# Re-ordering the start of an attention and feed-forward kernel: early scores, split zero fills, spreads ahead of a product, two more accumulator banks

## The chip, the cores and the metric

The kernel runs on one core of one Trainium2 chip. The metric is the device time of the whole program in microseconds, lower is better. A profile is one recorded execution of it; its times count from the first instruction of the span.

## What is computed

Causal attention over 4 batches, 8 heads, 768 positions and a head width of 64. Three heads ("retrieval", 0, 2 and 6) see all earlier keys. The other five ("streaming") see the first 4 keys (the sinks) and the last 64. The result, as a matrix of 3072 tokens by 512, goes through two matrix products with a leaky ReLU between them:

```python
scores = scale * np.matmul(q, k.transpose(0, 1, 3, 2))
mask = np.where(retr[0, :, 0, 0, None, None], full_mask, stream_mask)
scores = np.where(mask[None, :, :, :], scores, -1000000000.0)
a = np.exp(scores - np.max(scores, axis=-1, keepdims=True))
a = a / (np.sum(a, axis=-1, keepdims=True) + 1e-09)
attn_out = np.matmul(a, v)
x = np.ascontiguousarray(attn_out.transpose(0, 2, 1, 3)).reshape(B * S, H * D)
h = x @ w_in
out = np.maximum(0.01 * h, h) @ w_out
```

## The kernel before

The 3072 tokens are cut into eight chunks of 384 (`CH`), two for each batch. A chunk goes through three stages: attention, product 1 (`in_slots`: 16 ticks of four matmuls into a `ph` bank, evacuated by ACT with the leaky ReLU at L431) and product 2 (`out_slots`: three tiles of 128 tokens with 16 matmuls each, in parts of 3 or 4, copied by DVE at L447 and stored by SP).

The order on each engine is written out by hand. There is no scheduler that moves an instruction: the order of the Python calls is the order in which each engine gets its instructions. The tile layer adds a wait on a semaphore wherever an instruction touches data that another engine writes or reads, going by the regions that both touch. Each engine takes its instructions in that order, so one that waits holds all behind it.

Names used below:

- `kt[i]` holds the keys of a batch transposed, one plane for each pair of heads and each half of the pair (`hh`): the head's own 64 partitions hold keys, the other 64 partitions are zero, so that a matmul over all 128 partitions picks one head. `zero_keys` writes those zeros, for both chunks of the batch (768 positions). There are two such tiles, for batches in turn.
- Pairs: heads 0 and 1 are pair 0, and so on. R0, R2, R6 are the retrieval heads, S1, S3, S4, S5, S7 the streaming ones. `qk(*R0)` issues a head's score matmuls, its exponentials on ACT and its mask on DVE; `av(*R0)` multiplies by the values into an accumulator (`po` or `py` bank, by `po_tags`).
- `turn_pair(n, p, tags, engs)` transposes the keys and queries of pair p of chunk n on PE and copies them out of PSUM into `kt` and `qt` (L204 on DVE, L206 on ACT, by the letters `v` and `a`). Chunk 0's first two pairs come in fp32 by the DMA queues of SP and ACT (`kf`, `qf`); its other two come through Pool (`kw`, `qw`). Chunk 1's come through Pool (`kb`, `qb`) and are also turned on PE. From chunk 2 on the DMA transposes (`turn_dma`, into `kd` and `qd`), and `spreads` copies `kd` into `kt` on DVE (L228).
- `finish(p)` adds the sink part and normalises a pair on DVE into `xs` (L377, L379); `x_t` transposes `xs` on PE into `xt`, the input of product 1.
- `v_shift_pe` makes copies of the values shifted by 64 positions with a matmul by the matrix `shift`; `sink_keys`, `sink_values` and `a0.sink()` make the sink part.
- Pool issues the loads that convert to bf16 (`load_three`, `load_qk`, `load_v`, `load_in`, `load_out`) and builds the masks between them, all on one queue.

Chunk 0 runs alone at the start (`a0`). Then product 1 of chunk 0 (`p0`) and attention of chunk 1 (`a1`, slots of one score unit each, with its `av` two slots later and `x_t` three slots after the finish) are merged into one list. Product 1 of chunk 1 runs alone, then product 2 of chunks 0 and 1 (`o0`, `o1`) is merged with attention of chunk 2. From there a loop repeats the pattern for later chunks.

There are eight PSUM banks in four tags of two: `ph`, `psS`, `po`, `py`. A new tile of a tag waits until the one before the last of that tag has been read.

Of the kernel before, what the change touches and what calls it, by code (L numbers as in the profile page):

```python
# [13 lines left out]
ACTF = mybir.ActivationFunctionType  # L14
# [3 lines left out]
CH = 384  # L18
# [3 lines left out]
def kernel(  # L22
# [12 lines left out]
    nc = tc.nc  # L35
    B, H, S, D = q.shape
# [21 lines left out]
    def bf(name, *shape):  # L58
        return one.tile([128, *shape], BF16, name=name)
# [7 lines left out]
    ident = bf("ident", 128)  # L67
    ident_f = one.tile([128, 128], FP32, name="ident_f")
# [5 lines left out]
    shift = bf("shift", 2, 128)  # L74
    kt = [bf(f"kt{i}", 4, 2, S) for i in range(2)]
# [25 lines left out]
    def load_qk(n, nms="kq"):  # L101
        b, c = divmod(n, 2)
        for nm in nms:
            t = rot.tile([128, 3, H, D], BF16, name=f"{nm}b", tag=f"{nm}b", bufs=1)
            raw[nm, n] = t
            for g in range(3):
                nc.gpsimd.dma_start(out=t[:, g], in_=nat[nm][b, c, :, :, g])  # L107

    def load_v(n, gs=range(3)):
        b, c = divmod(n, 2)  # L110
        for g in gs:
            nc.gpsimd.dma_start(out=va[b % 2][:, 3 * c + g, :, 0:D], in_=nat["v"][b, c, :, :, g])  # L112
# [15 lines left out]
    def load_in(c0, c1):  # L128
        nc.gpsimd.dma_start(out=w_in_bf[:, :, c0:c1], in_=w_in_r[:, :, c0:c1])
# [13 lines left out]
    def v_shift_pe(t, tag, eng):  # L143
        s = bank(tag, [128, 512], FP32)
        w = 7 * (D + 1)
        for e in range(2):
            nc.tensor.matmul(s[:, 0:w], lhsT=shift[:, e, :], rhs=va[0][:, t + e, 1:H, :],
                             start=(e == 0), stop=(e == 1))
        dst, src = vb[0][:, t, 1:H, :], s[:, 0:w].rearrange("p (h d) -> p h d", h=7)
        if eng == "v":  # L150
            nc.vector.tensor_copy(dst, src)
        else:
            nc.scalar.activation(out=dst, in_=src, func=ACTF.Copy)
# [3 lines left out]
        nc.gpsimd.affine_select(out=m, in_=m, compare_op=comp, fill=0.0, base=base,  # L157
                                channel_multiplier=cm, pattern=pattern)

    def zero_keys(i, eng, hs=(0, 1)):  # L160
        for hh in hs:
            eng.memset(kt[i][64 - 64 * hh : 128 - 64 * hh, :, hh, :], 0.0)

    def zero_small(i, eng):
        eng.memset(ksink[i][:], 0.0)
# [13 lines left out]
    def turn_pair(n, p, tags, engs, nms="kq"):  # L179
        b, c = divmod(n, 2)  # L180
        i = b % 2
        if n not in qx:
            qx[n] = rot.tile([128, 4, CH], BF16, name="qt", tag="qt", bufs=2)
        for nm, tag, eng in zip(nms, tags, engs):
            f = n == 0 and p < 2
            pt = bank(tag, [128, 4, 128], FP32 if f else BF16)
            for g in range(3):
                if f:
                    nc.tensor.transpose(pt[:, g, :], three[nm, p, "f"][:, g], ident_f[:])  # L189
                elif n == 0:  # L190
                    for hh in range(2):
                        nc.tensor.transpose(pt[64 * hh : 64 * hh + 64, g, :],
                                            three[nm, 2 * p + hh][:, D * g : D * g + D], ident[:])
                else:
                    nc.tensor.transpose(pt[:, g, :], raw[nm, n][:, g, 2 * p : 2 * p + 2, :], ident[:])

            def move(dst, src):
                if n == 0 and not f:
                    src = src.rearrange("p g t -> p t g")
                    dst = dst.rearrange("p (t g) -> p t g", g=3)  # L200
                else:
                    dst = dst.rearrange("p (g t) -> p g t", g=3)
                if eng == "v":
                    nc.vector.tensor_copy(dst, src)  # L204
                else:
                    nc.scalar.activation(out=dst, in_=src, func=ACTF.Copy)  # L206

            if nm == "k":
                for hh in range(2):
                    r = slice(64 * hh, 64 * hh + 64)  # L210
                    move(kt[i][r, p, hh, CH * c : CH * c + CH], pt[r, 0:3, :])
            else:
                move(qx[n][:, p, :], pt[:, 0:3, :])
# [8 lines left out]
    def spreads(n):  # L222
        b, c = divmod(n, 2)

        def spread(g, hh):
            r = slice(64 * hh, 64 * hh + 64)
            o = CH * c + 128 * g
            nc.vector.tensor_copy(kt[b % 2][r, :, hh, o : o + 128], raw["kx", n][r, g])  # L228

        r = [lambda g=g, hh=hh: spread(g, hh) for g in range(3) for hh in range(2)]  # L230
        if c == 0:
            r += [lambda h=h: sink_key(b, h) for h in (1, 3, 5, 7, 4)]
        return r
# [4 lines left out]
    def into(slots, extra):  # L238
        r, extra = [], list(extra)
        for j, s in enumerate(slots):  # L240
            r.append(s)
            if 5 * j >= 2 * len(slots) and extra:
                r.append(extra.pop(0))
                if len(extra) > len(slots) - j - 2:
                    r.append(extra.pop(0))
        return r + extra
# [6 lines left out]
    def sink_keys(b):  # L253
        for h in (1, 3, 5, 7, 4):
            sink_key(b, h)
# [5 lines left out]
    class Attention:  # L261
# [13 lines left out]
        def av(self, p, hh, qi, lhsT, rhs):  # L275
            first = p not in self.po
            if first:
                self.po[p] = bank(self.po_tags[p], [128, 3, 2, D + 1], FP32)
            o = self.po[p][:, qi, :, :] if hh is None else self.po[p][:, qi, hh, :]
            nc.tensor.matmul(o, lhsT=lhsT, rhs=rhs, start=first, stop=False, skip_group_check=True)  # L280
# [140 lines left out]
    py = {}  # L421
# [39 lines left out]
    def run(*lists):  # L461
        for l in lists:
            for f in l:
                f()

    def merge(ms, as_):

        r, done = [], 0
        for j, m in enumerate(ms):
            want = (j + 1) * len(as_) // len(ms)  # L470
            r += as_[done:want] + [m]
            done = want
        return r + as_[done:]
# [6 lines left out]
    load_three("k", nc.gpsimd, 4, 8)  # L480
    load_three("q", nc.gpsimd, 4, 8)
    load_sinks(0)
    zero_keys(0, nc.vector, (0,))
    nc.vector.tensor_copy(ident_f[:], ident[:])
    zero_keys(0, nc.vector, (1,))
    nc.vector.memset(shift[:], 0.0)
    for i in range(2):
        nc.vector.memset(va[i][:, :, :, D], 1.0)
    for a in ats:
        nc.vector.memset(a[:, :, 1:3, :], 0.0)  # L490
    nc.gpsimd.memset(m_caus[:], 1.0)
    keep(m_caus[:], [[1, 128]], ALU.is_ge, 0, -1)
    load_v(0, (0,))
# [1 line left out]
    keep(m_one[:], [[-1, 64]], ALU.is_gt, 0, 1)  # L495
    keep(m_one[:], [[1, 64]], ALU.is_ge, 64, -1)
    load_v(0, (1, 2))
    nc.gpsimd.memset(m_sink[:], 1.0)
    keep(m_sink[:], [[-NS, H]], ALU.is_ge, 0, 1)
    keep(m_sink[:], [[NS, H]], ALU.is_ge, NS - 1, -1)  # L500
    zero_small(0, nc.gpsimd)
    load_in(0, 512)
    load_qk(1)
    load_in(512, 1024)
    load_v(1)
    load_in(1024, 2048)
# [5 lines left out]
    a0 = Attention(0, ("psS", "ph"), ("po", "po", "py", "py"))  # L512
    R0, S1, R2, S3, S4, S5, R6, S7 = (a0.units[h] for h in range(H))

    def qk(*us):
        run([x[0] for x in us])
# [2 lines left out]
        run([x[1] for x in us])  # L519

    turn_pair(0, 0, ("py", "py"), "va")
    turn_pair(0, 1, ("po", "po"), "av")
    nc.vector.tensor_copy(m_win[:], m_one.rearrange("p (o t) -> p o t", o=1).to_broadcast([128, 6, 64]))
    nc.vector.tensor_copy(m_win0[:, 1:], m_win[:, 1:])
    nc.vector.tensor_copy(m_win0[:, 0, :], m_caus[:, 0:64])
    nc.vector.memset(m_win0[0:NS, 1, :], 1.0)
    qk(*R0)
    turn_pair(0, 2, ("py", "py"), "va")
    qk(*S1)
    turn_pair(0, 3, ("po", "po"), "av")  # L530
    qk(*R2)
    qk(*S3)
    sink_keys(0)
    qk(*R6)
    nc.scalar.activation(out=shift[:, 0, 0:64], in_=ident[:, 64:128], func=ACTF.Copy)
    nc.scalar.activation(out=shift[:, 1, 64:128], in_=ident[:, 0:64], func=ACTF.Copy)
    sink_values(0, nc.vector)
    nc.vector.tensor_copy(vs[0][0:32, :, D], m_sink[0:32, :])
    qk(*S4)
    qk(*S5)  # L540
    av(*R0)
    qk(*S7)
    a0.sink()
    v_shift_pe(0, "psS", "a")
    av(*R2)
    v_shift_pe(1, "ph", "v")
    av(*R6)
    av(*S1)
    xs0 = a0.finish(0)
    av(*S3)  # L550
    xs1 = a0.finish(1)
    av(*S4)
    av(*S5)
    xs2 = a0.finish(2)
# [8 lines left out]
    p0 = in_slots(0)  # L563
# [3 lines left out]
    run(p0[1:2])  # L567
    turn_pair(1, 3, ("psS", "psS"), "va")
    run(p0[2:3])
    a1 = Attention(1, po_tags=("po", "po", "po", "py"), xt_eng="v").slots([0, 2, 6, 1, 3, 4, 5, 7])  # L570
    run(a1[0:2])
    turn_pair(1, 2, ("py", "py"), "va")
    v_shift(1)


    run(p0[3:4], merge(p0[4:8], a1[2:11]), merge(p0[8:14], a1[11:]), p0[14:])
    load_sinks(1)
    turn_dma(2)
    v_shift(2)
    load_qk(3)  # L580
    load_v(3)
    zero_keys(1, nc.vector)
    zero_small(1, nc.vector)
    nc.vector.tensor_copy(vs[1][0:32, :, D], m_sink[0:32, :])
    run(in_slots(1, ("ph",)))
# [3 lines left out]
    load_qk(4)  # L589
    load_v(4)  # L590
    o0, o1 = out_slots(0), out_slots(1)
    run(o0[0:6])
    run(spreads(2))
    run(merge(o0[6:] + o1[0:6], into(Attention(2).slots(), spreads(3))))
    outs = o1[6:]

    for n in range(2, NCH):
        a, extra = [], ()
# [10 lines left out]
        if n + 1 < NCH:  # L609
            a = into(Attention(n + 1).slots(), extra)  # L610
# [38 lines left out]
```

## Time and profile before

| | |
|---|---|
| device time, median of 3 | 245.46 us (245.42 to 247.18) |
| span of the profiled execution | 243.7 us |
| PE busy with matmuls | 227.6 us, 93% |
| ACT busy | 137.1 us, 56% |
| DVE busy | 98.3 us, 40% |
| Pool busy | 70.9 us, 29% |
| chain that ended last | PE 88%, ACT 4%, DVE 3%, DMA 2% |

PE is the engine with the largest share, and the chain of waits that ended last runs mostly through it. What PE is not busy with lies in a few stretches: 4.66 us before its first matmul, 3.2 us in the last 14 us, and the rest before 65 us. A line of a timeline gives the start and the duration in us, the engine, the line of the code, the operation with its output and inputs, the shapes and the count; the bracket at the end is the idle time of the engine just before it and what ended it. In a table of windows each engine has its busy time in that window, with the number of its instructions.

### The profile page before, as it was taken

Reading aid. Unit: us, or ns where it says so; the run is one execution under the profiler, and the core shown is the slowest. Engines: PE = TensorE matmul, PEld = TensorE weight load, DVE = VectorE, ACT = ScalarE, POOL = GpSimd, SP = SyncE. Lnnn points to the kernel's source line nnn. Section 1 sums busy time; section 2 is a strip of 40 time slices with the busy share of each in tenths; the row PEclk is TensorE's granted clock in tenths of the full one; section 3 lists DMA queues with packets and bytes.
Section 4 is the critical chain, followed back from the end, with each engine's and each line's share of the span. In section 5 each row is a group of like instructions: output and inputs, shape, how many; then the busy total and the mean of one; then the engine's idle time right before and its main releaser. Section 6 shows DMA issues by size and latency. Waiting matters only on the chain.

```text
span 243.7 us, 5022 instructions
## 1 busy us (share of the span) xinstructions
PE 227.6 (93%) x2024; PEld 137.9 (57%) x2024; DVE 98.3 (40%) x274; ACT 137.1 (56%) x302; POOL 70.9 (29%) x94
## 2 busy tenths in 40 slices
PE   2688987999799999999999999999999999999994
PEld 1456655554465666566556666566555666555553
DVE  7486317701686255516431473334421251211121
ACT  2485985572354777666557657565557667443300
POOL 6996523209357009539000580000000000000000
PEclk9999999999999999999999999999999999999999
DMA  7999999999999998999909598181110100111012
GB/s 129 136 166 177 205 233 196 156 182 108 117 216 195 167 184 58 163 207 160 132 0 159 120 138 86 60 180 46 43 43 4 43 28 18 43 46 43 29 60 86
DMA packets 100311, 27.79 MB, mean 114 GB/s; under 512 B 92608, under 2 KB 95936, under 8 KB 100288
## 3 DMA queue, kind: packets, MB, share of 16 engines
q0 software_dynamic: 73392, 13.24, 68.2%
q1 hardware_dynamic: 25296, 13.84, 26.5%
q10 hardware_dynamic: 1600, 0.39, 0.8%
q8 instruction: 16, 0.26, 0.4%
q14 instruction: 7, 0.06, 0.1%
HBM read 27.30 MB, written 6.29 MB: 138 GB/s over the span
## 4 chain that ended last, share of the span: by engine, by line
PE 88%; ACT 4%; DVE 3%; DMA 2%; issue 1%; SPq 1%
PE ph L429 34%; PE py L442 30%; PE po L280 7%; PE psS L311 5%; PE psS L442 4%; PE psS L346 2%; DMA kf<-in_k_dram 2%; PE psS L385 2%; PE psS L291 2%; ACT at L316 1%; DVE kt L228 1%; ACT kt L206 1%; PE po L189 1%; DVE xs L379 1%; SPq L99 1%
## 5 line engine op out<-in xcount | busy, mean ns | idle before, releaser
L429 PE MATMUL ph<-xt,w_in_bf 128*128 128x384 bf16 x512 | 101.8, 326 | 0.1
L431 ACT ACTIVATE g<-ph 128x384 bf16<-128x384 f32 x128 | 62.9, 492 | 55.9 <-PE ph L429 55.3
L442 PE MATMUL py<-w_out_bf,g 128*128 128x512 bf16 (+1 forms) x352 | 91.3, 374 | 0.0
L429 PEld LDWEIGHTS <-w_in_bf 128*128 128x128 bf16 x512 | 45.8, 97 | 30.1 <-issue 1.6
L442 PEld LDWEIGHTS <-g 128*128 128x128 bf16 x400 | 35.8, 98 | 26.3
L316 ACT ACTIVATE at<-psS 128x384 bf16<-128x384 f32 x81 | 38.8, 493 | 16.3 <-PE psS L311 15.2
L447 DVE COPY o<-py 128x512 f32<-128x512 f32 (+1 forms) x22 | 14.9, 677 | 42.5 <-PE py L442 42.5
L107 POOL DMA_DIRECT2D kb<-in_k_dram x21 | 18.7, 900 | 23.5 <-DMA kd<-kb 22.7
L112 POOL DMA_DIRECT2D va<-in_v_dram x24 | 21.4, 915 | 4.7 <-DVE linv L377 1.9
L311 PE MATMUL psS<-qd,kt 128*128 128x384 bf16 (+2 forms) x81 | 20.7, 291 | 1.6 <-DVE kt L228 1.6
L355 DVE TENSOR_TENSOR ats<-ats,m_win 128x384 bf16<-128x384 bf16 x40 | 14.0, 356 | 19.2 <-ACT ats L351 18.9
L107 POOL DMA_DIRECT2D qb<-in_q_dram x21 | 18.6, 913 | 8.0 <-PE py L280 4.6
L351 ACT ACTIVATE ats<-psS 128x384 bf16<-128x384 f32 x37 | 18.0, 492 | 3.6 <-PE psS L346 3.5
L321 DVE TENSOR_TENSOR at<-at,m_caus 128x128 bf16<-128x128 bf16 x24 | 6.0, 252 | 34.3 <-ACT at L316 34.2
L280 PEld LDWEIGHTS <-at 128*128 128x128 bf16 x252 | 16.0, 98 | 6.8 <-DVE at L321 1.0
L280 PE MATMUL po<-va,at 128*128 128x65 bf16 x231 | 19.3, 194 | 0.0
L379 DVE TENSOR_TENSOR xs<-po,linv 128x384 bf16<-128x384 f32 x29 | 16.2, 558 | 1.0
L311 PEld LDWEIGHTS <-kt 128*128 128x128 bf16 x108 | 10.4, 100 | 10.1 <-DVE kt L228 2.7
L346 PEld LDWEIGHTS <-kt 128*128 128x128 bf16 x240 | 12.0, 99 | 5.5 <-issue 0.7
L228 DVE COPY kt<-kd 64x512 bf16<-64x512 bf16 x36 | 14.8, 411 | 0.7
L387 ACT ACTIVATE xt<-psS 128x384 bf16<-128x384 bf16 x24 | 11.7, 488 | 5.6 <-PE psS L385 5.1
L280 PEld LDWEIGHTS <-ats 128*128 128x128 bf16 x240 | 11.3, 98 | 4.8 <-DVE xs L379 1.0
(103 smaller groups left out, 178.3 us busy)
## 6 DMA issues: line engine op xcount, KB each, us to landing
out_dram<-o SPq DMA_DIRECT2D x23, 256.0 KB, 2.9
va<-in_v_dram POOLq DMA_DIRECT2D x24, 128.0 KB, 6.7
kb<-in_k_dram POOLq DMA_DIRECT2D x21, 128.0 KB, 5.2
qb<-in_q_dram POOLq DMA_DIRECT2D x21, 128.0 KB, 6.4
w_out_bf<-in_moe_w_out_dram POOLq DMA_DIRECT2D x4, 512.0 KB, 17.8
vb<-va SPq DMA_DIRECT2D x8, 195.0 KB, 3.1
w_in_bf<-in_moe_w_in_dram POOLq DMA_DIRECT2D x2, 512.0 KB, 6.9
w_in_bf<-in_moe_w_in_dram POOLq DMA_DIRECT2D x1, 1024.0 KB, 13.5
```

Source lines behind the costliest of these rows:

```text
L107: nc.gpsimd.dma_start(out=t[:, g], in_=nat[nm][b, c, :, :, g])
L112: nc.gpsimd.dma_start(out=va[b % 2][:, 3 * c + g, :, 0:D], in_=nat["v"][b, c, :, :, g])
L228: nc.vector.tensor_copy(kt[b % 2][r, :, hh, o : o + 128], raw["kx", n][r, g])
L280: nc.tensor.matmul(o, lhsT=lhsT, rhs=rhs, start=first, stop=False, skip_group_check=True)
L311: nc.tensor.matmul(s[:, off : off + w], lhsT=kt[i][:, p, hh, 128 * kj : 128 * kj + 128], rhs=q_of(n, p, lo, CH), start=(j == 0), stop=(j = ...
L316: nc.scalar.activation(out=a[:, 0:off], in_=s[:, 0:off], func=ACTF.Exp, scale=SM)
L346: nc.tensor.matmul(s[:, 64 * m : 64 * m + 64], lhsT=kt[i][:, p, hh, k0 : k0 + 128], rhs=q_of(n, p, 64 * m, 64 * m + 64), start=(m == 0), s ...
L351: nc.scalar.activation(out=av_, in_=s[:, 0:CH].rearrange("p (j e f) -> p j e f", j=3, e=2), func=ACTF.Exp, scale=SM)
L379: nc.vector.tensor_tensor(xs[:], po[:, :, :, 0:D], linv.to_broadcast([128, 3, 2, D]), op=ALU.mult)
L429: nc.tensor.matmul(ph[:, 0:CH], lhsT=w_in_bf[:, g, 128 * t : 128 * t + 128], rhs=xts[n][:, g, :], start=(g == 0), stop=(g == KG - 1))
L431: nc.scalar.activation(out=gs[n][:, t, :], in_=ph[:, 0:CH], func=ACTF.Prelu, alpha=0.01)
L442: nc.tensor.matmul(py[n][:, 0 : c1 - c0], lhsT=gs[n][:, ng, 128 * tt : 128 * tt + 128], rhs=w_out_bf[:, ng, c0:c1], start=(ng == 0), stop= ...
```

## The change

The change re-orders the start of the kernel and three later places.

- The zero fill of the first `kt` is split. The part for chunk 0 stays on DVE; the part for chunk 1 (positions 384 to 767) goes to Pool, behind the loads of chunk 1's keys and queries. The small fills on DVE change places: the ones column of the values comes first. The two ACT copies that build `shift` move to the start.
- Chunk 0's first pair (R0 and S1) is scored as soon as it is turned, ahead of the turning of pair 1; the later pairs are likewise scored closer to where they are turned, and the sink, the shifts and the `av` calls change places.
- The first quarter of `w_in` is issued by Pool ahead of the sink mask and small fills.
- Chunk 1's attention uses two `po` and two `py` banks for its four accumulators, and the merge of its slots with product 1's ticks is cut differently, so that ticks 12 to 15 stand between its last three slots.
- The spreads of chunk 2's keys are issued on DVE ahead of product 2 of chunk 0, and chunk 2's attention starts one part of product 2 sooner.

They are meant to fill idle time of PE in the first 65 us. The same work is done; no operation is left out.

```diff
-    def zero_keys(i, eng, hs=(0, 1)):
-        for hh in hs:
-            eng.memset(kt[i][64 - 64 * hh : 128 - 64 * hh, :, hh, :], 0.0)
+    def zero_keys(i, eng, lo, hi):
+        for hh in range(2):
+            eng.memset(kt[i][64 - 64 * hh : 128 - 64 * hh, :, hh, lo:hi], 0.0)
...
-    zero_keys(0, nc.vector, (0,))
-    nc.vector.tensor_copy(ident_f[:], ident[:])
-    zero_keys(0, nc.vector, (1,))
-    nc.vector.memset(shift[:], 0.0)
     for i in range(2):
         nc.vector.memset(va[i][:, :, :, D], 1.0)
+    nc.vector.memset(shift[:], 0.0)
+    nc.vector.tensor_copy(ident_f[:], ident[:])
+    zero_keys(0, nc.vector, 0, CH)
     for a in ats:
         nc.vector.memset(a[:, :, 1:3, :], 0.0)
+    nc.scalar.activation(out=shift[:, 0, 0:64], in_=ident[:, 64:128], func=ACTF.Copy)
+    nc.scalar.activation(out=shift[:, 1, 64:128], in_=ident[:, 0:64], func=ACTF.Copy)
...
     load_v(0, (1, 2))
+    load_in(0, 512)
     nc.gpsimd.memset(m_sink[:], 1.0)
...
     zero_small(0, nc.gpsimd)
-    load_in(0, 512)
     load_qk(1)
+    zero_keys(0, nc.gpsimd, CH, S)
     load_in(512, 1024)
...
     turn_pair(0, 0, ("py", "py"), "va")
-    turn_pair(0, 1, ("po", "po"), "av")
...
     qk(*R0)
+    qk(*S1)
+    turn_pair(0, 1, ("po", "po"), "av")
     turn_pair(0, 2, ("py", "py"), "va")
-    qk(*S1)
-    turn_pair(0, 3, ("po", "po"), "av")
     qk(*R2)
     qk(*S3)
+    turn_pair(0, 3, ("po", "po"), "av")
     sink_keys(0)
     qk(*R6)
-    nc.scalar.activation(out=shift[:, 0, 0:64], in_=ident[:, 64:128], func=ACTF.Copy)
-    nc.scalar.activation(out=shift[:, 1, 64:128], in_=ident[:, 0:64], func=ACTF.Copy)
+    qk(*S4)
+    a0.sink()
     sink_values(0, nc.vector)
     nc.vector.tensor_copy(vs[0][0:32, :, D], m_sink[0:32, :])
-    qk(*S4)
+    av(*R0)
     qk(*S5)
-    av(*R0)
+    v_shift_pe(0, "psS", "a")
+    v_shift_pe(1, "ph", "v")
+    av(*R2)
     qk(*S7)
-    a0.sink()
-    v_shift_pe(0, "psS", "a")
-    av(*R2)
-    v_shift_pe(1, "ph", "v")
-    av(*R6)
     av(*S1)
     xs0 = a0.finish(0)
     av(*S3)
     xs1 = a0.finish(1)
+    av(*R6)
     av(*S4)
...
-    a1 = Attention(1, po_tags=("po", "po", "po", "py"), xt_eng="v").slots([0, 2, 6, 1, 3, 4, 5, 7])
+    a1 = Attention(1, po_tags=("po", "po", "py", "py"), xt_eng="v").slots([0, 2, 6, 1, 3, 4, 5, 7])
...
-    run(p0[3:4], merge(p0[4:8], a1[2:11]), merge(p0[8:14], a1[11:]), p0[14:])
+    run(p0[3:4], merge(p0[4:8], a1[2:11]), merge(p0[8:12], a1[11:-3]), merge(p0[12:], a1[-3:]))
...
-    zero_keys(1, nc.vector)
+    zero_keys(1, nc.vector, 0, S)
...
-    run(o0[0:6])
     run(spreads(2))
-    run(merge(o0[6:] + o1[0:6], into(Attention(2).slots(), spreads(3))))
+    run(o0[0:5])
+    run(merge(o0[5:] + o1[0:6], into(Attention(2).slots(), spreads(3))))
```

## What I predict for the change

> **What bounds the kernel now.** First the busy shares at the head of the page, then a table of windows that shows where the bound engine idles:
>
> ```profile
> PE 227.6 (93%) x2024; PEld 137.9 (57%) x2024; DVE 98.3 (40%) x274; ACT 137.1 (56%) x302; POOL 70.9 (29%) x94
> ```
>
> ```profile
> core 0: us, PE busy (x) PEld busy (x) DVE busy (x) ACT busy (x) POOL busy (x), PEclk, DMA share, GB/s
> 5.00:10.00 5.00, 2.88 (x13) 2.06 (x12) 1.94 (x7) 1.29 (x3) 4.67 (x12) 1.00 1.72 177
> 10.00:15.00 5.00, 4.66 (x62) 3.25 (x60) 4.52 (x14) 4.50 (x12) 5.00 (x6) 1.00 1.16 131
> 20.00:25.00 5.00, 4.00 (x37) 2.63 (x37) 3.52 (x11) 3.85 (x9) 2.71 (x5) 1.00 1.81 179
> 30.00:45.00 15.00, 12.66 (x162) 8.65 (x161) 7.69 (x22) 9.87 (x24) 4.75 (x6) 1.00 1.48 205
> 45.00:59.90 14.90, 14.90 (x83) 7.88 (x82) 2.65 (x6) 8.41 (x18) 6.17 (x8) 1.00 1.70 147
> 59.90:65.00 5.10, 3.45 (x29) 1.76 (x28) 4.48 (x15) 1.49 (x4) 3.19 (x4) 1.00 2.52 155
> 65.00:230.00 165.00, 165.00 (x1465) 98.93 (x1462) 62.39 (x172) 98.33 (x215) 33.60 (x38) 1.00 0.76 96
> ```
>
> From 65 us on PE never stops, so nothing there can be gained. The change can only win idle PE time before 65 us: 2.12 us at 5-10, about 2 us spread over 10-25, 2.34 us at 30-45 and 1.65 us at 59.9-65. PE works in order, so it reduces to two questions: when does the first tick of product 1 (`p0[0]`, 22.20 us) start, and how much idle is left between it and 65 us? The PE timeline names the later gaps:
>
> ```profile
> 39.54 0.20 PE L280 MATMUL po<-vb,ats 128*128 128x65 bf16 x1 [0.89 <-DVE xs L379]
> ...
> 42.90 0.34 PE L385 MATMUL psS<-ident,xs 128*128 128x128 bf16 x3 [0.58 <-DVE xs L379]
> ```
>
> The first is the third `po` accumulator waiting for one of two banks to be normalised, the second a transpose waiting for xs. The gap at 59.9-65 is told by DVE:
>
> ```profile
> 59.88 0.69 DVE L447 COPY o<-py 128x512 f32<-128x512 f32 x1 [11.80 <-PE py L442]
> 60.49 3.09 DVE L228 COPY kt<-kd 64x512 bf16<-64x512 bf16 x6
> ```
>
> The spreads stand behind an output copy that waits for PE; PE then waits 0.33 and 1.32 us for them.
>
> **What the Trainium skill says.** "PSUM — Partial Sum Buffer", Engine vs sequencer instructions: the queues of ScalarE, VectorE and GpSimdE are strict FIFO. The fence above agrees: ready spreads stood 11.8 us behind a copy. "TensorE: Matmul & The Clock Gate", What's actually happening: the array runs at half rate after an idle window of about 3.4 us and returns to full rate after a busy one, the window being free-running. The trace agrees with a half-rate start: a 128x384 score at 12.60 us took 0.50 us, the one at 13.94 us 0.32, and the six 64-wide score matmuls went from 0.40-0.50 to 0.34. "VectorE: DVE Perf Modes", Zero memsets can be issued as uint32: a memset costs a cycle per element, so a Vector zero fill counts half the bf16 elements. Agreed: 64x1536 uint32 took 1.34 us for 3072 bf16. "GPSIMD Engine Reference", Elementwise — side-by-side cycle accounting: about 1.03 cycles per element in a simple loop. Pool fills of 8, 64, 128 and 512 bf16 took 0.13, 0.17, 0.20-0.23 and 0.52 us, 0.78 ns per element.
>
> **The change part by part.**
>
> *Head, up to pair 1.* R0 and S1 go to PE straight after pair 0: qt ends at 6.70 us, so they run at about 6.75-7.9, in the 2.1 us in which PE waited for kf. That takes about 1.2 us of half-rate PE work and, with the two shift copies, five ACT operations (3 x 0.39 + 2 x 0.15 = 1.5 us) out of the dense stretch from 9.2 us. DVE's first fills halve (1.34 to about 0.70 each); the mask copies run in DVE's gap before 9 us. Alone: about 1.5 us earlier. va's ones come first on DVE, so Pool loses its wait of 1.33 us at 5.04.
>
> *The fill moved to Pool.* `zero_keys(0, gpsimd, CH, S)` stands on Pool behind `load_qk(1)`. In the built program's list of waits, the DVE copy of pair 2's keys into kt (chunk 0, L204) and ACT's copy of pair 3's now wait for the second of these two Pool fills; the copies of pairs 0 and 1 do not, and none did before. Pool before:
>
> ```profile
> 9.01 0.52 POOL L165 MEMSET ksink<- 128x512 bf16 x1
> ...
> 13.31 2.66 POOL L107 DMA_DIRECT2D qb<-in_q_dram  x3
> 15.95 0.78 POOL L129 DMA_DIRECT2D w_in_bf<-in_moe_w_in_dram  x1
> ```
>
> qb's issues end at 15.95. Less the 1.33 us (w_in's issue only changes places ahead of them) that is 14.62. Two fills of 1536 bf16: 0.13 + 1528 x 0.78 ns = 1.33 us each, 2.63 together (0.9 to 2 us each would be my bounds: DVE's rate, and 1.5 times the slope). The fills end at 17.25. The pair-2 copy started at 11.79, so DVE stands some 5.5 us, and in-order behind it are the masks of R2 and S3 and qt of pair 3:
>
> ```profile
> 11.79 1.11 DVE L204 COPY kt<-py 64x384 bf16<-64x384 bf16 x2
> 12.94 0.36 DVE L355 TENSOR_TENSOR ats<-ats,m_win 128x384 bf16<-128x384 bf16 x1
> 13.33 0.56 DVE L204 COPY qt<-po 128x384 bf16<-128x384 bf16 x1
> ```
>
> ACT's wait holds pair 3's kt copy, and behind it R6's exponentials, which could not run sooner anyway. R6's scores need that qt: 17.25 + 0.05 + 1.11 + masks 0.23 + 0.29 + 0.36 + 0.56 = 19.85 us, against 13.94. PE runs out of work at about 12.75 (8.28 + transposes 1.7 + 0.85, R2 0.7, S3 0.4, transposes 0.85) and idles 7.1 us, long enough to fall to half rate by the skill.
>
> *From R6 to product 1.* Before, x_t(0) started at 19.52 and p0[0] 2.68 us later, paced by four normalisations on DVE; I keep 2.68. If PE is at full rate, DVE sets the pace after R6: exp 1.1, masks 0.52, S4 0.36, sink values 0.90, S5 0.36, vb 0.63, S7 0.36, reciprocal and xs 0.76 = 5.0, x_t(0) at 24.85. At half rate PE does: R6 0.61, S4 0.4, sink 4 x 0.215, av 0.42, S5 0.4, shifts 4 x 0.38, av 0.42, S7 0.4 = 5.0, then S7's exp 0.65, mask 0.36, reciprocal and xs 0.76: 26.65; if the clock returns midway, 25.9. I take 26.2: **+6.7 us** at x_t(0) and so at p0[0] (28.9), the head's gain already inside.
>
> *Merge of product 1 with chunk 1 and four accumulators.* Pair 2 goes to a py bank: the 0.89 us gap goes. Ticks now stand between the last transposes: the 0.58 goes. The ACT waits of 0.36 and 0.45 stay (same exp stream), perhaps 0.1 worse. **-1.4 us.**
>
> *Spreads ahead of product 2.* The key transpose was issued at 46.3 us and only waited for kb's data; qd landed at 54.5. DVE is idle from 48 to 59.9, so spreads of 3.1 us end well ahead of PE. **-1.65 us.**
>
> *w_in sooner, other Pool loads 1.3 us later* (w_in's second part issues at 17.25 instead of 15.95): no cost, the DMA engines are full from 12.4 to 48 us with that queue, and PE comes later than its data anyway.
>
> Sum: 6.7 - 1.4 - 1.65 = +3.65, 245.46 + 3.6 = 249.1.
>
> **The rivals.**
> (B) The wait is there, but PE stays warm, or DVE gets through its list faster: +5.3 at x_t(0), total +2.25: 247.7, about the 1% bound. For: PE's list overlaps DVE's. Against: 7 us of idle.
> (C) More is lost: fills of 2 us each (+1.3), or the merged tail gives only half its 1.4: 250.5 to 251.
> (D) The fills do not hold anything, as if done by 11 us: head -1.5, merge -1.4, spreads -1.65: 240.9. Against: they stand behind six load issues of 0.9 us on Pool, and the wait is written in the program.
> (E) Part of both: a stall of 3 us or less, +0: 245.5.
>
> **How the numbers follow.** Forecast 249.1: 45%; B 25%; C 20%; D 5%; E 5%. Slower by over 1% means above 247.91: 38 of the 45, 10 of B's 25, all of C's: 68%. Faster: D, 5%. The rest, 27%, within 1%. Range: from 246.3, between E and B, to 251.4, C with both of its losses; it leaves out D, E and a tail.
>
> **What would show it.** Pool: two kt fills ending near 17.3. DVE: idle of some 6 us before L204 kt<-py, released by Pool. PE: idle of some 7 us near 13-20, first 128x384 score after it at 0.50 us. p0[0] near 28.9. No waits for xs near the end of product 1 and none for kt in product 2. Wrong if DVE passes pair 2's copy before 14 us, if p0[0] comes before 26, or if a new wait appears after it.

## The result, and the profile after

| | before | after |
|---|---|---|
| device time, median | 245.44 us (245.37 to 247.18) | 249.51 us (249.33 to 249.75) |
| ratio after to before, 95% interval | | 1.0149 [1.0104, 1.0195] |
| span of the profiled execution | 243.7 us | 248.0 us |
| first tick of product 1, `p0[0]` | 22.20 us | 29.36 us |

The changed kernel is slower by 1.5%. The busy shares at the head of the page of after, and PE's rows in the 40 slices of the span (busy tenths, then the granted clock in tenths):

```profile
PE 226.9 (91%) x1995; PEld 139.2 (56%) x2024; DVE 97.1 (39%) x274; ACT 137.7 (56%) x302; POOL 73.9 (30%) x96
...
PE   2707898999999999999999999999999999999994
...
PEclk9965999999999999999999999999999999999999
...
PE 86%; POOL 7%; ACT 3%; DVE 3%; issue 1%; POOLq 0%
```

PE's busy time is about that of before (29 of its 2024 matmuls left no record in this profile), but its row now has a zero in the third slice (12.4 to 18.6 us). The last line is the chain that ended last: Pool was not among its four largest shares before, and now has 7%. The table of windows of after:

```profile
core 0: us, PE busy (x) PEld busy (x) DVE busy (x) ACT busy (x) POOL busy (x), PEclk, DMA share, GB/s
...
10.00:15.00 5.00, 2.13 (x33) 1.52 (x31) 0.49 (x1) 1.97 (x5) 4.96 (x7) 0.99 1.82 181
15.00:20.00 5.00, 0.00 (x0) 0.10 (x1) 2.20 (x6) 0.97 (x2) 4.95 (x5) 0.50 1.74 110
20.00:25.00 5.00, 4.79 (x45) 3.39 (x45) 3.75 (x13) 2.68 (x6) 4.79 (x7) 0.50 1.81 175
...
30.00:45.00 15.00, 13.85 (x156) 9.20 (x154) 3.96 (x13) 13.25 (x32) 7.37 (x9) 1.00 1.45 206
```

At 15-20 us PE does nothing, and its clock stands at 0.50 through 15-25 us. DVE too is nearly idle at 10-15 us (0.49 us of work, where before it had 4.52). At 30-45 us PE is idle for 1.15 us, before for 2.34; but PE's work comes 7 us later, so the two windows do not cover the same work, and the two later gains are measured further down, from one piece of work to another. What holds DVE is read in the timeline of after, all engines:

```profile
12.19 2.66 POOL L107 DMA_DIRECT2D qb<-in_q_dram  x3
14.89 2.80 POOL L162 MEMSET kt<- 64x1536 bf16 x2
17.72 0.99 ACT L206 ACTIVATE kt<-po 64x384 bf16<-64x384 bf16 x2 [5.32 <-POOL kt L162]
17.72 1.12 DVE L204 COPY kt<-py 64x384 bf16<-64x384 bf16 x2 [7.22 <-POOL kt L162]
...
19.60 0.56 DVE L204 COPY qt<-po 128x384 bf16<-128x384 bf16 x1
...
20.21 0.48 PE L311 MATMUL ph<-qt,kt 128*128 128x384 bf16 x1 [8.08 <-DVE qt L204]
...
29.36 0.88 PE L429 MATMUL ph<-xt,w_in_bf 128*128 128x384 bf16 x4
```

The brackets are to be followed from the bottom up. R6's score (20.21) waited 8.08 us for `qt`. Its copy (19.60) stood on DVE behind the copy of pair 2's keys, which waited 7.22 us for Pool's fill, and that fill stood behind three query loads. The score took 0.48 us: half rate.

### The profile page after: what moved, and what is told of

It reads as the page before. It is cut to its first block, busy times and chain, and to the rows that moved or that the text cites. A ratio compares the mean times of both kernels' runs of the same rounds, so it can differ in the third digit from the quotient of the medians.

```text
span 248.0 us, 4997 instructions
## 1 busy us (share of the span) xinstructions
PE 226.9 (91%) x1995; PEld 139.2 (56%) x2024; DVE 97.1 (39%) x274; ACT 137.7 (56%) x302; POOL 73.9 (30%) x96
## 4 chain that ended last, share of the span: by engine, by line
PE 86%; POOL 7%; ACT 3%; DVE 3%; issue 1%; POOLq 0%
PE ph L429 33%; PE py L442 29%; PE po L280 6%; PE psS L311 5%; PE psS L442 3%; PE psS L346 2%; PE psS L385 2%; PE psS L291 2%; POOL kt L162 1%; POOL qb L107 1%; POOL kb L107 1%; POOL va L112 1%; DVE xs L379 1%; ACT at L316 1%; DVE ats L355 1%
## 5 line engine op out<-in xcount | busy, mean ns | idle before, releaser
L442 PE MATMUL py<-w_out_bf,g 128*128 128x512 bf16 (+1 forms) x324 | 86.2, 374 | 1.4
L316 ACT ACTIVATE at<-psS 128x384 bf16<-128x384 f32 x81 | 38.9, 493 | 13.4 <-PE psS L311 12.4
L311 PEld LDWEIGHTS <-kt 128*128 128x128 bf16 x108 | 10.4, 99 | 16.5 <-ACT kt L206 6.3
L107 POOL DMA_DIRECT2D qb<-in_q_dram x21 | 18.6, 915 | 0.9 <-DMA w_out_bf<-in_moe_w_out_dram 0.9
L379 DVE TENSOR_TENSOR xs<-po,linv 128x384 bf16<-128x384 f32 x28 | 15.6, 558 | 1.0
L346 PEld LDWEIGHTS <-kt 128*128 128x128 bf16 x240 | 12.6, 102 | 5.7 <-issue 0.9
L319 DVE TENSOR_TENSOR at<-at,m_caus 128x256 bf16<-128x256 bf16 x24 | 7.0, 292 | 17.9 <-ACT at L316 17.9
L228 DVE COPY kt<-kd 64x512 bf16<-64x512 bf16 x36 | 13.5, 374 | 0.6
```

What stands on the lines that cost most here:

```text
L311: nc.tensor.matmul(s[:, off : off + w], lhsT=kt[i][:, p, hh, 128 * kj : 128 * kj + 128], rhs=q_of(n, p, lo, CH), start=(j == 0), stop=(j = ...
L316: nc.scalar.activation(out=a[:, 0:off], in_=s[:, 0:off], func=ACTF.Exp, scale=SM)
L346: nc.tensor.matmul(s[:, 64 * m : 64 * m + 64], lhsT=kt[i][:, p, hh, k0 : k0 + 128], rhs=q_of(n, p, 64 * m, 64 * m + 64), start=(m == 0), s ...
L379: nc.vector.tensor_tensor(xs[:], po[:, :, :, 0:D], linv.to_broadcast([128, 3, 2, D]), op=ALU.mult)
L442: nc.tensor.matmul(py[n][:, 0 : c1 - c0], lhsT=gs[n][:, ng, 128 * tt : 128 * tt + 128], rhs=w_out_bf[:, ng, c0:c1], start=(ng == 0), stop= ...
```

## The experiments

Two things had to be told apart: what of the loss is the wait itself and what the cold PE behind it; and whether the other parts give what the sum says. Times are medians; "ratio" is to the kernel before, timed together with the version, with its 95% interval. A "cold" PE is one at half rate, a "warm" one is at full rate. Places within a kernel (`p0[0]` and the like) come from one profiled run of each version. Of the twelve expectations below only those of e3, e4 and e5 came out in their range; every other version took longer than its theory said, e14 and e15 by only 0.1 us more than their range.

**e1: no wait, fill still on Pool.** The fill is cut by pair, so that no fill spans several pairs.

```diff
         for hh in range(2):
-            eng.memset(kt[i][64 - 64 * hh : 128 - 64 * hh, :, hh, lo:hi], 0.0)
+            for ps_ in ((slice(0, 4),) if eng is nc.vector else [slice(p, p + 1) for p in range(4)]):
+                eng.memset(kt[i][64 - 64 * hh : 128 - 64 * hh, ps_, hh, lo:hi], 0.0)
```

> The changed kernel, with Pool's two fills of the second half of kt cut into eight, one for each pair and half: the same bytes at the same place on Pool's queue, but the copies of pairs 2 and 3 no longer carry a wait for them. Theory (the wait on the fill is the loss): DVE passes the copy of pair 2 near 11 us, PE has no gap near 12 to 20 us, p0[0] near 20.7 us, time 240.9 us (239.5 to 242.5). Rival 1 (the loss is Pool's later loads, not the wait): the fills still take 2.8 us or a little more of Pool, so 249.5 us or up to 0.3 more. Rival 2 (DVE or ACT bound the head anyway): the gap goes but only half of it is won, about 245 us.

**e2: fill of positions 384 to 767 on DVE**, behind S1's mask.

```diff
     load_qk(1)
-    zero_keys(0, nc.gpsimd, CH, S)
...
     qk(*S1)
+    zero_keys(0, nc.vector, CH, S)
     turn_pair(0, 1, ("po", "po"), "av")
```

> The changed kernel, with the fill of the second half of kt on DVE, behind the mask of S1, where DVE stood idle from 8.6 to 9.9 us. Two fills of 0.70 us. Theory: no wait on Pool, qt of pair 1 comes some 0.2 us later, time 241.1 us, within 0.6 us of the version with eight fills on Pool. Rival (Pool's loads 2.8 us later cost time themselves): this one is faster than the version with eight fills by 1 us or more.

**e4: fill later on Pool**, behind two more sets of loads.

```diff
     load_qk(1)
-    zero_keys(0, nc.gpsimd, CH, S)
     load_in(512, 1024)
     load_v(1)
+    zero_keys(0, nc.gpsimd, CH, S)
```

> The changed kernel, with Pool's two fills behind the loads of w_in's second part and of v of chunk 1 (four issues, 0.76 + 2.68 us). Theory (the wait on the fill): the fills end 3.4 us later, near 21.1 us, R6's scores and p0[0] move by as much, time 252.9 us (252.3 to 253.5). Rival (the later loads behind the fill are the loss): 249.5 us or less, as these loads now come sooner.

**e3: after, with PE kept busy while it waits**, by 36 matmuls of 128x384 whose result nobody reads.

```diff
     sink_keys(0)
+    warm = bank("psS", [128, 512], FP32)
+    for j in range(36):
+        nc.tensor.matmul(warm[:, 0:CH], lhsT=kt[0][:, 0, 0, 0:128], rhs=qx[0][:, 0, :], start=(j == 0), stop=(j == 35))
     qk(*R6)
```

> The changed kernel, with 36 extra matmuls of 128x384 into a spare bank ahead of R6's scores (5.8 us at full rate, done before R6 may start), so that PE does not idle there; their result is not used. Theory (half rate after the idle time costs 1.4 of the 7.2 us): R6 still starts near 20.2 us, its first score takes 0.33 us instead of 0.48, x_t(0) follows 5.0 us after R6 instead of 6.5, time 248.1 us (247.7 to 248.6). Rival (DVE sets the pace after the stall at either rate): 249.5 us.

| | time | ratio | `p0[0]` |
|---|---|---|---|
| e1, fills by pair | 244.89 us | 0.9966 [0.9952, 0.9980] | 22.57 us |
| e2, fill on DVE | 242.82 us | 0.9901 [0.9865, 0.9938] | 22.81 us |
| e4, fill later | 252.99 us | 1.0305 [1.0290, 1.0320] | 32.44 us |
| e3, PE kept busy | 247.73 us | 1.0091 [1.0076, 1.0106] | 27.47 us |

*The wait is the cause.* Without it `p0[0]` is back near 22.7 us; with the fill moved back, everything moves with it. The timeline of e4:

```profile
18.14 2.80 POOL L162 MEMSET kt<- 64x1536 bf16 x2
...
20.98 1.12 DVE L204 COPY kt<-py 64x384 bf16<-64x384 bf16 x2 [10.04 <-POOL kt L162]
...
23.47 0.48 PE L311 MATMUL ph<-qt,kt 128*128 128x384 bf16 x1 [10.50 <-DVE qt L204]
```

The fill came 3.25 us later, R6 3.26 us later, the end 3.48 us later, although two sets of the loads that had stood behind the fill now came sooner: so those loads are not the loss. It is a wait without a need: the fill writes positions 384 to 767 and the held copies write chunk 0's 0 to 383. In e1 the fills still end only at 17.78 us and hold nobody. Why a fill over four pairs held the copies of pairs 2 and 3 but not those of 0 and 1 wasn't settled; the copies of 2 and 3 are written with another pattern of the tile.

*What the cold PE costs.* PE's timeline of e3:

```profile
12.73 6.02 PE L538 MATMUL psS<-qt,kt 128*128 128x384 bf16 x36
...
20.08 0.32 PE L311 MATMUL ph<-qt,kt 128*128 128x384 bf16 x1 [1.32 <-DVE qt L204]
```

R6 starts 0.13 us sooner than in after and takes 0.32 us in place of 0.48; `p0[0]` comes 1.89 us sooner and the end 1.78 us sooner. So of the 7.16 us by which `p0[0]` slipped, about 1.9 is the half rate after the wait.

*Without the wait the head gains nothing.* 22.57 and 22.81 us lie behind the 22.20 of before. PE's timeline of e1 shows why:

```profile
10.99 0.50 PE L312 MATMUL psS<-qt,kt 128*128 128x384 bf16 x1
...
13.82 0.48 PE L312 MATMUL ph<-qt,kt 128*128 128x384 bf16 x1 [0.91 <-DVE qt L205]
...
15.58 0.54 PE L281 MATMUL po<-va,at 128*128 128x65 bf16 x6
...
17.70 0.35 PE L281 MATMUL po<-va,at 128*128 128x65 bf16 x6
```

R2's score does come 1.6 us sooner (10.99 us, before 12.60). R6 stands where it stood before (13.94): pair 3 is now turned behind R2 and S3, and PE waits 0.91 us for the copy of its queries. And R6 is at half rate: 0.48 us against 0.32. Six 128x65 matmuls take 0.54 us at 15.58 and 0.35 at 17.70, so the first half-rate phase lasted to about 17.7 us in this run; in the profiled run of before it was over by 13.9.

*e1 is 2.07 us behind e2, though its `p0[0]` is no later.* DVE and SP's queue in e1, near chunk 3's keys:

```profile
61.25 2.14 SPq L220 DMA_TRANSPOSE kd<-kb  x1
...
69.60 0.28 DVE L229 COPY kt<-kd 64x512 bf16<-64x512 bf16 x1 [3.14 <-DMA kd<-kb]
```

and in e2:

```profile
58.62 1.52 SPq L219 DMA_TRANSPOSE kd<-kb  x1
...
67.09 0.28 DVE L228 COPY kt<-kd 64x512 bf16<-64x512 bf16 x1 [0.38 <-DMA kd<-kb]
```

With the fills (3.1 us) on Pool, chunk 3's keys are transposed 2.6 us later, and DVE waits 3.14 us in its spreads. Masks stand behind these: e1 has waits of PE for `ats` of 1.3 us, 0.9 the longest, and PE is idle for 1.45 us at 65-75 us, in e2 for 0.11. The chain that ended last agrees: in e1 18% of the span in it is DMA, most of that the loads and transposes of keys; in e2 it is 3%. How the 3.1 us on Pool grow into these 2.6 us was not followed load by load.

**e5 and e6: the two later parts alone**, each on the kernel before.

```diff
     o0, o1 = out_slots(0), out_slots(1)
-    run(o0[0:6])
     run(spreads(2))
-    run(merge(o0[6:] + o1[0:6], into(Attention(2).slots(), spreads(3))))
+    run(o0[0:5])
+    run(merge(o0[5:] + o1[0:6], into(Attention(2).slots(), spreads(3))))
```

> The kernel before, with only the spreads of chunk 2 issued ahead of product 2 and chunk 2's attention one part sooner. Theory (the 1.65 us of idle near 60.5 to 63.3 us is all that it wins): time 243.8 us (243.4 to 244.3), no wait of PE for kt<-kd. Rival (the next wait takes its place, since chunk 3's key transpose comes no sooner and its spreads stand in the same DVE queue ahead of masks): 244.5 to 245.5 us, with DVE waiting for kd near 67 to 70 us.

```diff
-    a1 = Attention(1, po_tags=("po", "po", "po", "py"), xt_eng="v").slots([0, 2, 6, 1, 3, 4, 5, 7])
+    a1 = Attention(1, po_tags=("po", "po", "py", "py"), xt_eng="v").slots([0, 2, 6, 1, 3, 4, 5, 7])
...
-    run(p0[3:4], merge(p0[4:8], a1[2:11]), merge(p0[8:14], a1[11:]), p0[14:])
+    run(p0[3:4], merge(p0[4:8], a1[2:11]), merge(p0[8:12], a1[11:-3]), merge(p0[12:], a1[-3:]))
```

> The kernel before, with only the two accumulators in py banks and the new merge of product 1 with chunk 1's slots. Theory: the waits of 0.89 and 0.58 us for xs near 39.5 and 42.9 us go, time 244.1 us (243.6 to 244.6). Rival (the exponentials on ACT set the pace of that stretch): 245.0 us or more.

| | time | ratio | saved |
|---|---|---|---|
| e5, spreads ahead | 244.25 us, 20 runs, 243.55 to 245.30 | 0.9945 [0.9932, 0.9959] | 1.29 us |
| e6, merge and accumulators | 244.93 us, 20 runs, 243.93 to 245.49 | 0.9973 [0.9963, 0.9984] | 0.61 us |

In e5 the wait for `kt` in product 2 is gone, but a new one stands in PE's waits:

```profile
PE po L280 <- DVE ats L355: 1.2, 2, 0.8
```

It is at 65-75 us, as the rival had it, and looks like e1's: DVE waits 3.05 us for chunk 3's keys, where in after it waits for none of them. The profiled execution was the slowest of the 20; the other 19 left no trace, so the 1.2 us is likely more than most of them lost. In e6 PE's waits have:

```profile
PE psS L385 <- DVE xs L379: 0.2, 1, 0.2
```

The waits for `xs` of 0.89 and 0.58 us fall to 0.2, and the spreads' wait stays (1.7 us), as it should. PE's idle time at 30-45 us falls from 2.34 to 1.38 us: 0.96, not 1.4, since waits for ACT remain.

What each part is worth can be read between three places of the same work: `p0[0]`, ACT's evacuation of the last tick of product 1 of chunk 1, and the seventh output copy of product 2. The lines of before, and then of after:

```profile
56.43 0.49 ACT L431 ACTIVATE g<-ph 128x384 bf16<-128x384 f32 x1 [0.25 <-PE ph L429]
...
110.42 0.68 DVE L447 COPY o<-py 128x512 f32<-128x512 f32 x1
...
62.88 0.49 ACT L431 ACTIVATE g<-ph 128x384 bf16<-128x384 f32 x1 [0.25 <-PE ph L429]
...
114.74 0.68 DVE L447 COPY o<-py 128x512 f32<-128x512 f32 x1
```

| profiled run of (us) | `p0[0]` | last tick, chunk 1 | seventh copy | first stretch | second stretch |
|---|---|---|---|---|---|
| before | 22.20 | 56.43 | 110.42 | 34.23 | 53.99 |
| after | 29.36 | 62.88 | 114.74 | 33.52 | 51.86 |
| e2 | 22.81 | 56.33 | 108.19 | 33.52 | 51.86 |
| e1 | 22.57 | 56.08 | 109.97 | 33.51 | 53.89 |
| e5 | 21.75 | 56.35 | 110.32 | 34.60 | 53.97 |
| e6 | 22.28 | 55.80 | 110.02 | 33.52 | 54.22 |

Behind the seventh copy all six take the same time to their last copy. The merge and the accumulators win 0.71 us in the first stretch, in after, e1, e2 and e6 alike. The spreads win 2.13 us in the second, in after and e2; in e1 and in the slowest run of e5, where DVE waits for chunk 3's keys, they win nothing. Of the 2.13 us 1.65 is the wait that the prediction named; the rest is not located. e1's lag behind e2 lies in the second stretch (2.03 us). The sooner `p0[0]` of e5 is lost again in its first stretch, where PE waits 0.3 us for `w_in`.

**e9, e10: the head without the wait, then also warm.** e9 puts the fill on DVE after chunk 1's third pair is turned. e10 adds 46 matmuls of 128x128 whose result nobody reads (26 ahead of the first transposes, 4 before R0, 8 after S1, 8 before R6).

```diff
     turn_pair(1, 2, ("py", "py"), "va")
+    zero_keys(0, nc.vector, CH, S)
     v_shift(1)
```

> The changed kernel, with the fill of the second half of kt on DVE behind the turning of chunk 1's pairs, where DVE is less loaded, instead of on Pool. Theory (with no fill ahead of R6 the head is as the change meant it): R6 near 13.0 us instead of 13.8, p0[0] at 22.0 to 22.3 us, time 242.2 us (241.5 to 242.8). Rival (PE at half rate until its first full busy window, not DVE, paces the head from R6 on): p0[0] stays at 22.5 us or later, 242.8 us.

```diff
+    def warm(k):
+        s = bank("psS", [128, 512], FP32)
+        for j in range(k):
+            nc.tensor.matmul(s[:, 0:128], lhsT=ident[:], rhs=ident[:], start=(j == 0), stop=(j == k - 1))
+
+    warm(26)
     turn_pair(0, 0, ("py", "py"), "va")
...
+    warm(4)
     qk(*R0)
     qk(*S1)
+    warm(8)
     turn_pair(0, 1, ("po", "po"), "av")
...
+    warm(8)
     qk(*R6)
```

> The version with the late fill on DVE, with extra 128x128 matmuls into spare banks in PE's idle places of the first 13 us (26 before the first transposes, 4 before R0, 8 after S1, 8 before R6); their results are not used. Theory (the head's expected 1.5 us was lost to half rate lasting until near 18 us instead of 13.9): scores take 0.33 us from about 8 us on, p0[0] near 20.7 us, time 240.8 us (240.2 to 241.6). Rival (ACT and DVE pace the head): no change against the version without the extra matmuls, 242.2 us.

e9 took 243.04 us, 0.9891 [0.9853, 0.9929], `p0[0]` at 21.28 us; e10 242.51 us, 0.9870 [0.9837, 0.9902], `p0[0]` at 19.90 us. In e10 the first score runs at full rate:

```profile
5.76 0.32 PE L311 MATMUL ph<-qt,kt 128*128 128x384 bf16 x1 [0.35 <-ACT qt L206]
```

A warm PE makes the re-ordered head 2.3 us earlier than before; the old head with the same warming wasn't tried. e9 shows the next bound: `p0[0]` is 1.5 us sooner than in e2, and the time no better. PE waits 0.6 us for the late fill, and is idle for 0.74 us at 65-75 us (0.11 in e2); DVE waits there again for chunk 3's keys, 2.43 us.

**e12 to e15: chunk 3's spreads later.** Each starts `spreads(3)` at 80% of chunk 2's slots and not at 40%, so that DVE does not stand waiting for them: e12 is e10 with it, e13 e9, e15 e1, and e14 the kernel before with both late parts.

```diff
-    def into(slots, extra):
+    def into(slots, extra, k=2):
...
-            if 5 * j >= 2 * len(slots) and extra:
+            if 5 * j >= k * len(slots) and extra:
...
-    run(merge(o0[5:] + o1[0:6], into(Attention(2).slots(), spreads(3))))
+    run(merge(o0[5:] + o1[0:6], into(Attention(2).slots(), spreads(3), 4)))
```

> The version with the late fill on DVE and the extra matmuls, with the spreads of chunk 3 moved to the last slots of chunk 2's attention (from 40% to 80% of its slots). Theory (chunk 3's keys come from the DMA transpose at a time that the head does not move, and their spreads block DVE ahead of chunk 2's masks): PE's waits of about 0.9 us near 65 to 75 us go, time 241.5 us (240.9 to 242.1). Rival (the DMA itself is the bound, wherever the spreads stand): 242.5 us.

> The version with the late fill on DVE, without extra matmuls, with the spreads of chunk 3 moved likewise. Theory: the waits near 65 to 75 us go, 242.3 us (241.6 to 243.0), 0.8 us or more above the same with extra matmuls, as p0[0] comes 1 us or more later. Rival: 243.0 us.

> The kernel before with both later parts (spreads of chunk 2 ahead of product 2, two py accumulators and the new merge) and the spreads of chunk 3 moved likewise; the head, the fills and the order of the weights are as before. Theory (the changed head without its wait wins nothing, as p0[0] stays near 22 us): 242.3 us (241.7 to 243.0), as fast as the changed head with its fill on DVE. Rival (the changed head is worth about 1 us): 243.3 us.

> The version with eight fills on Pool, with the spreads of chunk 3 moved likewise. Theory (its 2 us above the version with the fill on DVE came from DVE waiting 3.1 us for chunk 3's transposed keys, whose loads Pool issued 3 us later): 242.9 us (242.3 to 243.5). Rival (Pool's later loads cost in another place): 244.5 us or more.

| | time | ratio |
|---|---|---|
| e12, on e10 | 242.54 us | 0.9872 [0.9853, 0.9890] |
| e13, on e9 | 243.80 us, 8 runs, 242.02 to 244.78 | 0.9912 [0.9879, 0.9945] |
| e14, head of before and both late parts | 243.07 us | 0.9890 [0.9875, 0.9906] |
| e15, on e1 | 243.62 us | 0.9910 [0.9891, 0.9928] |

By the medians only e15 gains, 1.27 us on e1, and e12 equals e10. The profiled runs say how. In e13 and e14 PE waits for no mask of chunks 2 and 3 any more. In e12 the wait only moves on, to where DVE waits 2.61 us for the keys of chunk 4; this is PE's timeline of e12, and then of e15:

```profile
87.11 0.20 PE L280 MATMUL po<-vb,ats 128*128 128x65 bf16 x1 [0.85 <-DVE ats L355]
...
63.56 0.22 PE L281 MATMUL po<-vs,at_sink 128*128 128x65 bf16 x2 [0.63 <-POOL vs L122]
```

So in e12 the arrival of keys is still what is waited for, as its rival had it. In e15 PE waits 0.63 us for the sink values that Pool makes (`vs`) and 0.43 us for a mask near 88 us, and the second stretch of the table takes 53.67 us, hardly less than e1's 53.89. But `p0[0]` is at 21.78 us in its profiled run, 0.79 us sooner than in e1's, with the same head. Those two runs are 1.00 us apart, so most of that comes from the head, and it is not shown that the place of the spreads was e1's lag.

e13's runs lie in two groups, 242.0 to 243.2 and 244.4 to 244.8 us, so its median says nothing about the spreads. In its profiled run `p0[0]` is at 22.91 us, in e9's at 21.28, though both have the same head. PE's timeline of e9:

```profile
13.89 0.32 PE L311 MATMUL ph<-qt,kt 128*128 128x384 bf16 x1 [0.90 <-DVE qt L204]
```

and of e13:

```profile
13.77 0.48 PE L311 MATMUL ph<-qt,kt 128*128 128x384 bf16 x1 [0.91 <-DVE qt L204]
...
17.70 0.54 PE L280 MATMUL po<-va,at 128*128 128x65 bf16 x6
```

R6 starts within 0.12 us of the same time, at full rate in the one and at half rate in the other, where six 128x65 matmuls still take 0.54 us at 17.70 (in e9 0.35 at 15.03). So the same head comes out in two ways, some 1.6 us apart at `p0[0]`, and the difference is when PE reaches full rate. This is likely what makes the two groups; only one run of each has a trace, so it isn't shown for the rest.

e14 answers the question that matters most: with the old head, the kernel is within 0.3 us of e2. It also has chunk 3's spreads moved, and the two late parts without that move were not run together. But the table above says the same of e2's profiled run: its `p0[0]` is 0.61 us later than before, and all that it wins comes behind that. So the gain of the repaired version comes from the late parts; the re-ordered head is not seen to add to it, and where its `p0[0]` did come sooner (e9, e15), the median was no better than e2's. With PE warmed it may: e12 is 0.53 us below e14, both with the spreads moved, but their intervals overlap.

The best versions beat both kernels: e10 and e12 at 242.5 us, and e2 at 242.8 without extra matmuls.

## Why the prediction was right, point by point

- **The fill's end.** Predicted 17.25 us, measured 17.69: qb's issues ended 0.23 us later and the two fills took 2.80 us in place of 2.63. The duration from the slope of smaller Pool fills was good to 6%.
- **Who waits.** This was read from the waits of the built program; from the data alone no wait was due. DVE's copy of pair 2 was to stand some 5.5 to 6 us; it stood 7.22, since DVE reached it at 10.50 us and not at 11.79. R6 was predicted at 19.85 and came at 20.21.
- **From R6 to product 1.** The choice between full and half rate was the largest free number. The 26.2 us for x_t(0) was picked between the sums for a late and an early return of the clock; it came at 26.68, and `p0[0]` at 29.36 against 28.9. At full rate the working had 5.0 us from R6 to x_t(0), e3 took 4.72; in after it took 6.47. The clock column shows 0.50 at 15-25 us, and e3 priced it at 1.8 us of the time. "TensorE: Matmul & The Clock Gate", What's actually happening, has half rate after an idle window of about 3.4 us; 8.08 us of idle agrees. Rival B, PE staying warm, was given 247.7 us; e3, which makes it so, took 247.73.
- **The later gains.** Predicted 3.05 us; in the profiled run of after they are 2.84, so the sum is nearly right, but by luck: the merge won 0.71 us and not 1.4, the spreads 2.13 and not 1.65, and the two errors nearly cancel. For the merge the working took out both waits for `xs` and let the waits for ACT grow by 0.1 us at most; in e6 one more wait for ACT (0.34 us) came, and 0.17 us of waiting for `xs` stayed. By the medians e5 alone won 1.29 us and e6 alone 0.61. In after PE is 7 us late at this place, and chunk 3's keys are there in time. In e5 PE is there at the time of before, and DVE waits 3.05 us for the keys; in e2 PE is there at the same time as in e5, but the keys are transposed 1.3 us sooner (58.62 us against 59.93), and DVE waits only 0.38. The working's "spreads of 3.1 us end well ahead of PE" looked at chunk 2's keys only, and not at what the freed PE would meet next.
- **"Alone: about 1.5 us earlier"** for the head was wrong: `p0[0]` came 0.4 and 0.6 us later than before in the profiled runs of e1 and e2, 0.4 and 0.9 us sooner in those of e15 and e9. It missed two things. It carried the time won ahead of pair 1 on to product 1, but R6 did not move (13.8 to 13.9 us in e1, e2, e9 and e13): it waits for pair 3, which now stands behind R2 and S3. And it took the half-rate phase as ending where it ended before; e13 against e9 shows that it may not, with the same head. Rival D, 240.9 us without the wait, inherits the error: the runs without it took 242.8 to 244.9 us. With a warm PE (e10) `p0[0]` gains 2.3 us.
- **The other Pool loads, 1.3 us later at "no cost"**, were not tested alone. In after no such cost is seen, as PE comes late itself. In e1, where it does not, 2.03 us are lost where DVE waits for later keys.
- **Rival C's sum.** Half of the merge's 1.4 lost is 0.7, so that 249.8 us belongs to it alone, not 250.5; with both of its losses it is 251.1 and not 251.4. The merge did win only about half.

So the forecast was right by its main terms, the wait and the cold clock behind it, which e1 to e4 show. The later gains were right as a sum only, and the head's 1.5 us and the loads' cost did not show, since the stall covered them.

## What to carry to other kernels

Before a piece of work is moved to a lightly loaded engine, look at what stands ahead of it in that engine's queue, and in the built program at who waits for it: here a fill made two engines stand for 5 to 7 us, though it shares no element with the copies that it held. Cutting the fill into one part for each pair removed the wait without moving the work. A long gap of PE can cost twice: the one of 8.08 us cost its own length and then 1.8 us of half-rate work. And a wait that is removed may only hand over to the next: in e5, e9, e10 and e12 DVE then waited 2.2 to 3.1 us for the keys of chunk 3 or chunk 4.

## What was not expected of the hardware

- The granted clock in the windows shows the half rate after the stall (0.50 at 15-25 us of after) but not the one at the start: it reads 1.00 at 5-15 us of before, where a 128x384 score takes 0.50 us.
- When the first half-rate phase ends is not fixed by the kernel: with the same head it ended before 13.9 us in the profiled run of e9, and after 18 us in that of e13 (six 128x65 matmuls took 0.54 us at 17.70). "TensorE: Matmul & The Clock Gate", What's actually happening, says that the window is free-running, so that the moment varies by some 0.5 us with it, and that one busy window of about 3.4 us is enough. The moment varied here by over 4 us. PE has gaps of 0.25 to 0.9 us between 8 and 14 us in both runs; that a window with such gaps counts as busy in one position and not in another would explain it, and wasn't tested.
